# A three-stage fp32 network on one core: w1 loaded a second time for its sums, and fixed places for splits, sums and conversions

## The chip, the cores and the metric

The kernel runs on one core of one Trainium2 chip. Its engines are named as in the profile: PE (TensorE, matrix multiplication; PEld is its weight load), DVE (VectorE), ACT (ScalarE), POOL (GpSimd) and SP (SyncE, which issues most DMAs). Each engine works through its own queue in the order in which the program wrote the instructions, and waits on semaphores for the others. The metric is the device time in microseconds. Three runs before gave 1493.35 in the median (1492.63 to 1495.95).

## The reference: what is computed

Three layers follow one another, all in float32.

```python
# 1. attention, B=2, H=8, S=768, D=64; keep = first n_sink keys or a causal window of 128
scores = where(keep, q @ k.T / sqrt(D), -1e9)
x = softmax(scores) @ v                      # then rows of 8 heads side by side: x is 1536 x 512
# 2. mixture of E=8 experts, every token through each of them
P = exp(x @ w_gate - max); 8 times: P /= row sums, P /= column sums, P *= N/E
x = sum_e P[:, e] * (relu(x @ w1[e]) @ w2[e])     # w1[e] 512 x 1024, w2[e] 1024 x 512
# 3. one more two-layer network, d_ff = 2048; its weights arrive as 64-bit floats
out = (relu(x @ w_in) ** 2) @ w_out
```

## The kernel before

**Numbers.** Every float32 operand of a matmul is split in two parts, a high part in the type fp32r and the rest (lo = x - hi), and each product is three matmuls (hi x lo, hi x hi, lo x hi) that add up in one PSUM bank. `pair_split` (L428) makes a split: ACT copies to the high part, POOL subtracts.

**Chunks.** Behind attention, the two networks are 20 chunks of 512 hidden columns: chunk 0 is woven into attention, chunks 1 to 15 are the experts, 16 to 19 the last network. For a chunk, PE computes h = relu(x w1) for three blocks of 512 tokens (t = 0, 1, 2) and then adds h w2 into the accumulator `acc`. The order in PE's queue is: first products for t = 0 and 1; `second(c, 1)` (four groups of 12 matmuls); `plain(c, 2, f)` (four groups, the first products of t = 2); `second(c, 0)` and `second(c, 2)` (eight groups).

**Fast products.** Chunks 2 to 15 and 17 to 19 compute t = 0 and 1 with Strassen's scheme in Winograd's form (`fast`, L721): 7 products of 6 matmuls instead of 8, for each half of the chunk's columns, so 14 products p1, p6, p5, p2, p7, p3, p4, twice. It needs sums of w1's blocks (S1 to S4) and of x's blocks (T1 to T4, made once by `sums`, L604, for the experts and once for the last network). Within a half, p1's result is copied by ACT ("ts", L745), and DVE adds p6's to it ("tu"), p5's to that ("tz"), and so on (L737). p2 adds into the bank that "ts" has read, and p3 into the bank that "tz" has read, so PE waits for these two.

**Weights.** Raw weights come by DMA into a ring of three buffers of 512 KB (`rawp`), in the order of `load_list` (L388). A load is written into the queue as soon as the load three places ahead in the list has been used (`next_loads`, L400). A w1 half (`half_w1`, L432) is split in two steps into the tiles g0h, g0l (or g1h, g1l), then four POOL additions (L456) make the sums in place in the raw buffer, and two more splits follow. So the second splits wait for the sums, and the buffer is free only after them. `half_w2` (L466) does the two halves of w2.

**64-bit weights.** `wide` (L480) turns a piece of the last network's weights into float32: eight DVE operations (L491 to L519) on the tiles x0 and x1, and a DMA back to DRAM ("w<-x", L520). 32 pieces, three a chunk from chunk 2 on. L496, the second operation, writes x1, which the DMA of the piece before still reads.

**Order around the change.** All is written out by hand. `run` (L1197) takes a list of groups; after each group it takes `side` steps from a list of generators (`todo`) and some conversion steps, and after every second one a step of the gate (`gate`, L826). The w2 splits stand in the first groups of a chunk, the w1 splits of the next chunk in its last eight groups, two steps after each, and what is left over is written out at the end of the chunk. The conversion has three steps in two groups over the last 16 groups.

**Accumulation.** `add_up` (L574) adds a group's result into `acc` on DVE; in chunk 2 it multiplies `acc` by P first (L584). In the last chunk each tile of 128 tokens is stored right after it.

Of the kernel before, what the change touches and what calls it, by code (L numbers as in the profile page):

```python
# [2 lines left out]

# [15 lines left out]
DM = H * D  # L19
# [18 lines left out]
CONV = 3  # L38
NB = 512
# [5 lines left out]
class Kernel:  # L45
# [354 lines left out]
    def next_loads(self, *used):  # L400

        self.used.add(used)
        while self.lk < len(self.loads):
            if self.lk >= 3 and self.loads[self.lk - 3] not in self.used:
                return
            c, which, half = k = self.loads[self.lk]
            self.lk += 1
            if which == 2:
                raw = self.rawp.tile([128, 2 * FC], I32, tag="raw", name="raw64")
                w = (self.w1, self.w2)[c // 4 % 2][NC1 + c // 8]  # L410
                src = w[:, c % 4].bitcast(I32)
            else:
                w = self.w32[c - NC1, which] if c >= NC1 else (self.w1, self.w2)[which][c]
                if which == 0:
# [17 lines left out]
    def half_w1(self, c, half):  # L432

        nc = self.nc
        raw = self.loaded(c, 0, half)
        g = tuple(
            self.w1p.tile([128, 8, 2, 128], F32R, tag=f"g{half}{t}", name=f"g{half}{t}")
            for t in "hl"
        )
        self.W[c, half] = g  # L440
        parts = [
            tuple(x[:, k : k + 2].rearrange("p u k f -> p (u k) f") for x in g)
            for k in (0, 2, 4, 6)
        ]
        srcs = [raw[:, :, 0:128], raw[:, :, 128:256]]
        for k in range(2):
            self.pair_split(*parts[k], srcs[k])
            yield
        if self.is_fast(c):
            a11, a12 = raw[:, 0:2, 0:128], raw[:, 2:4, 0:128]  # L450
            a21, a22 = raw[:, 0:2, 128:256], raw[:, 2:4, 128:256]
            for o, x, y, op in (
                (a22, a21, a22, ALU.add), (a21, a11, a21, ALU.subtract),
                (a11, a22, a11, ALU.subtract), (a12, a12, a11, ALU.subtract),
            ):
                nc.gpsimd.tensor_tensor(out=o, in0=x, in1=y, op=op)  # L456
                yield
            for k in range(2):
                self.pair_split(*parts[2 + k], srcs[k])
                yield  # L460
        self.next_loads(c, 0, half)
# [4 lines left out]
    def half_w2(self, c, half):  # L466
        raw = self.loaded(c, 1, half)
        if half == 0:
# [3 lines left out]
        w = self.W[c, 2]  # L472
        for k in range(2):
            self.pair_split(w[0][:, 2 * half + k], w[1][:, 2 * half + k], raw[:, k])
            if k == 0:
                yield
        self.next_loads(c, 1, half)
        yield
# [95 lines left out]
    def add_up(self, c, ti, ps):  # L574

        nc = self.nc
        a = self.acc[:, ti, :]
# [13 lines left out]
        if c == NC - 1:  # L591
            nc.sync.dma_start(out=self.out[ti * 128 : (ti + 1) * 128, :], in_=a)
# [11 lines left out]
    def sums(self):  # L604
# [18 lines left out]
        for kc in range(2):  # L623
# [5 lines left out]
            yield  # L629
            x = tt("z", f32("B12", 0, kc), f32("B11", 0, kc), ALU.subtract)  # L630
# [87 lines left out]
    def weight(self, c, half, k):  # L718
        return tuple(x[:, k] for x in self.W[c, half])
# [63 lines left out]
    def second(self, c, t):  # L783

        def group(k):
            def go():
                s = slice(128 * k, 128 * k + 128)
                hh, hl = self.h[c, t]
                wh, wl = self.W[c, 2]
                ps = self.mmtile()  # L790
                n = 0
                for f in (0, 1, 3, 2):
                    for x, w in ((hh, wh), (hh, wl), (hl, wh)):
                        self.nc.tensor.matmul(  # L794
                            out=ps, lhsT=x[:, f, s], rhs=w[:, f], start=(n == 0), stop=(n == 11)
                        )
                        n += 1
                self.add_up(c, 4 * t + k, ps)
                self.finish()
            return go  # L800
# [169 lines left out]
    def reset(self):  # L970
# [6 lines left out]
        self.wr, self.W, self.h = {}, {}, {}  # L977
# [167 lines left out]
    def phase_b(self, c0, first, fill):  # L1145
# [27 lines left out]
        todo = [self.half_w1(c0, half) for half in range(2)]  # L1173

        def side_step():
            while todo:
                try:
                    return next(todo[0])
                except StopIteration:
                    todo.pop(0)  # L1180
# [6 lines left out]
        while todo:  # L1187
            side_step()
# [8 lines left out]
        def run(seq, side=1, conv=0):  # L1197
            for g in seq:
                g()
                for _ in range(side):  # L1200
                    side_step()
# [10 lines left out]
        for c in range(c0, NC):  # L1212
            if c == 2:
                for _ in gate:
                    pass
                self.steps = conv
            if not low:
                seq = [self.plain(c, 1, 0), *rest]
                run(seq)
# [9 lines left out]
            todo += [self.half_w2(c, half) for half in range(2)]  # L1229
# [3 lines left out]
            run(seq)  # L1233
            while todo:
                side_step()
            if c in (FAST - 1, FAST2 - 1):
                todo.append(self.sums())
            run(self.second(c, 1) + [self.plain(c, 2, f) for f in range(KD)], conv=3)
            if c + 1 < NC:
                todo += [self.half_w1(c + 1, half) for half in range(2)]  # L1240
            seq = self.second(c, 0) + self.second(c, 2)
            if c == NC1 - 1:
                x = [self.x2(t, kc) for t in (1, 0) for kc in range(KD)]
                seq = sum(([s, x[k]] for k, s in enumerate(seq)), [])
            run(seq, 2, 3)
            while todo:
                side_step()
# [94 lines left out]
```

## Time and profile before

| | |
|---|---|
| median of three runs | 1493.35 us |
| profiled execution | 1492.53 us, of which the span from the first to the last instruction 1490.7 us |
| PE busy | 1420.8 us (95%) |
| DVE busy | 848.1 us (57%) |
| POOL busy | 509.3 us (34%) |
| ACT busy | 449.0 us (30%) |
| mean granted clock of PE | 0.982 |
| read from HBM, written | 71.85 MB, 11.53 MB |

Matmuls are pipelined: the profile gives a matmul of 512 columns some 0.39 us, but the next one starts 0.23 us after it, so the distance between starts tells more than the length. PE counts as busy as long as one of them runs. The granted clock is a share of 2.4 GHz; 0.5 of it is the lower level, 1.2 GHz. A name such as "ts" or "hh" in a row is the tile that is written, without its buffer's number. In a row of a timeline, the brackets hold the idle time ahead of the instruction and what ended it.

### The profile page before, as it was taken

Reading aid. Unit: us, or ns where it says so; the run is one execution under the profiler, and the core shown is the slowest. Engines: PE = TensorE matmul, PEld = TensorE weight load, DVE = VectorE, ACT = ScalarE, POOL = GpSimd, SP = SyncE. Lnnn points to the kernel's source line nnn. Section 1 sums busy time; section 2 is a strip of 40 time slices with the busy share of each in tenths; the row PEclk is TensorE's granted clock in tenths of the full one; section 3 lists DMA queues with packets and bytes.
Section 4 is the critical chain, followed back from the end, with each engine's and each line's share of the span. In section 5 each row is a group of like instructions: output and inputs, shape, how many; then the busy total and the mean of one; then the engine's idle time right before and its main releaser. Section 6 shows DMA issues by size and latency. Waiting matters only on the chain.

```text
span 1490.7 us, 17219 instructions
## 1 busy us (share of the span) xinstructions
PE 1420.8 (95%) x6587; PEld 1169.5 (78%) x6587; DVE 848.1 (57%) x1567; ACT 449.0 (30%) x925; POOL 509.3 (34%) x461
## 2 busy tenths in 40 slices
PE   5799999999999999999999999999999999899998
PEld 4688888787778787878778787878888888678886
DVE  7978823866655546555565656554342446555352
ACT  5667622222221212122221212222122233334231
POOL 4534311535061423416152342515325021704320
PEclk9899999999999999999999999999999999999999
DMA  3322120012220312122131212212010010101001
GB/s 113 113 60 86 42 72 29 5 58 66 71 91 30 99 43 78 57 86 84 37 99 33 88 57 85 75 46 78 15 43 29 29 57 1 50 7 57 15 23 66
DMA packets 43181, 84.60 MB, mean 57 GB/s; under 512 B 3664, under 2 KB 25168, under 8 KB 42832
## 3 DMA queue, kind: packets, MB, share of 16 engines
q1 hardware_dynamic: 42800, 83.39, 17.6%
q8 instruction: 54, 0.88, 0.3%
q14 instruction: 39, 0.32, 0.1%
q10 hardware_dynamic: 288, 0.00, 0.0%
HBM read 71.85 MB, written 11.53 MB: 56 GB/s over the span
## 4 chain that ended last, share of the span: by engine, by line
PE 65%; DVE 13%; POOL 9%; DMA 6%; ACT 4%; issue 3%; ACTq 0%; DVEq 0%; SPq 0%; POOLq 0%
PE mm L794 28%; PE mm L696 27%; DMA raw<-w 5%; POOL raw L456 4%; POOL g1l L430 3%; PE xp L353 3%; POOL g0l L430 2%; PE mm L564 2%; PE mm L539 2%; DVE hl L674 1%; PE sc L225 1%; DVE hl L680 1%; DVE p L265 1%; DVE tx L668 1%; ACT hh L679 1%
## 5 line engine op out<-in xcount | busy, mean ns | idle before, releaser
L794 PE MATMUL mm<-w2h,hh 128*128 128x512 f32 x912 | 357.3, 392 | 0.8 <-ACT hh L679 0.8
L794 PE MATMUL mm<-w2h,hl 128*128 128x512 f32 x912 | 356.2, 391 | 0.0
L794 PE MATMUL mm<-w2l,hh 128*128 128x512 f32 x912 | 355.7, 390 | 0.0
L430 POOL TENSOR_TENSOR g0l<-raw,g0h 128x512 fp32r<-128x512 f32 x72 | 92.5, 1307 | 546.9 <-ACT g0h L429 546.9
L588 DVE SCALAR_TENSOR_TENSOR acc<-mm,P,acc 128x512 f32<-128x512 f32 x168 | 125.3, 746 | 173.7 <-PE mm L794 173.0
L794 PEld LDWEIGHTS mm<-w2h,hh 128*128 128x128 f32 x912 | 171.7, 188 | 37.2 <-ACT hh L679 2.1
L794 PEld LDWEIGHTS mm<-w2h,hl 128*128 128x128 f32 x912 | 171.5, 188 | 37.1 <-DVE hl L680 1.3
L794 PEld LDWEIGHTS mm<-w2l,hh 128*128 128x128 f32 x912 | 171.7, 188 | 35.4
L663 ACT ACTIVATE hh<-mm 128x512 fp32r<-128x512 f32 x96 | 57.2, 596 | 323.1 <-PE mm L696 323.1
L696 PE MATMUL mm<-xl,g1h 128*128 128x512 f32 x320 | 126.9, 397 | 20.5 <-ACT ts L745 20.4
L696 PE MATMUL mm<-xl,g0h 128*128 128x512 f32 x320 | 126.8, 396 | 11.3 <-ACT ts L745 6.9
L430 POOL TENSOR_TENSOR w2l<-raw,w2h 128x512 fp32r<-128x512 f32 x76 | 97.7, 1307 | 103.5 <-ACT w2h L429 103.5
L696 PE MATMUL mm<-xh,g0l 128*128 128x512 f32 x320 | 125.7, 393 | 0.0
L696 PE MATMUL mm<-xh,g0h 128*128 128x512 f32 x320 | 125.6, 393 | 0.0
L696 PE MATMUL mm<-xh,g1h 128*128 128x512 f32 x320 | 125.3, 392 | 0.0
L696 PE MATMUL mm<-xh,g1l 128*128 128x512 f32 x320 | 125.2, 391 | 0.0
L456 POOL TENSOR_TENSOR raw<-raw 128x256 f32<-128x256 f32 x136 | 120.5, 886 | 10.7
L430 POOL TENSOR_TENSOR g1l<-raw,g1h 128x512 fp32r<-128x512 f32 x72 | 96.8, 1365 | 69.0 <-ACT g1h L429 63.8
L674 DVE SCALAR_TENSOR_TENSOR hl<-mm,hh 128x512 fp32r<-128x512 f32 x96 | 65.8, 685 | 66.5 <-ACT hh L663 66.2
L429 ACT ACTIVATE g1h<-raw 128x512 fp32r<-128x512 f32 x72 | 41.5, 623 | 181.1 <-POOL raw L456 113.7
L696 PEld LDWEIGHTS mm<-xl,g1h 128*128 128x128 f32 x320 | 60.4, 189 | 37.8 <-ACT ts L745 24.7
L696 PEld LDWEIGHTS mm<-xl,g0h 128*128 128x128 f32 x320 | 60.6, 189 | 25.6 <-ACT ts L745 8.4
(199 smaller groups left out, 2400.4 us busy)
## 6 DMA issues: line engine op xcount, KB each, us to landing
raw<-w SPq DMA_DIRECT2D x76, 512.0 KB, 4.3
raw<-win SPq DMA_DIRECT2D x16, 512.0 KB, 4.8
w<-x SPq DMA_DIRECT2D x32, 256.0 KB, 4.5
raw<-wout SPq DMA_DIRECT2D x16, 512.0 KB, 5.3
raw<-qkv SPq DMA_DIRECT2D x8, 624.0 KB, 3.8
raw<-qkv SPq DMA_DIRECT2D x8, 464.0 KB, 3.5
out<-acc SPq DMA_DIRECT2D x12, 256.0 KB, 2.0
wraw<-w SPq DMA_DIRECT2D x2, 1024.0 KB, 7.8
```

Source lines behind the costliest of these rows:

```text
L225: nc.tensor.matmul(out=ps[:, 0:wd], lhsT=x[r, l * 128 : (l + 1) * 128], rhs=y[r, QW + off : QW + off + wd], start=(m == 0), stop=(m == 2),)
L353: nc.tensor.matmul(out=o, lhsT=l, rhs=r, start=(k == 0), stop=(k == last), skip_group_check=True)
L429: self.nc.scalar.activation(out=hi, in_=src, func=AF.Copy)
L430: self.nc.gpsimd.tensor_tensor(out=lo, in0=src, in1=hi.bitcast(F32), op=ALU.subtract)
L456: nc.gpsimd.tensor_tensor(out=o, in0=x, in1=y, op=op)
L539: nc.tensor.matmul(out=ps[:, 0:n], lhsT=w[:, kc, f * 128 : (f + 1) * 128], rhs=x[:, kc, t0 : t0 + n], start=(k == 0), stop=(k == 3 * KD - 1),)
L564: nc.tensor.matmul(out=ps, lhsT=x[:, f, s], rhs=w[:, f, :], start=(k == 0), stop=(k == 3 * KD - 1),)
L588: nc.vector.scalar_tensor_tensor(out=a, in0=ps, scalar=self.P[:, ti, e : e + 1], in1=a, op0=ALU.mult, op1=ALU.add)
L663: nc.scalar.activation(out=hh, in_=src, func=AF.Relu)
L674: nc.vector.scalar_tensor_tensor(out=hl, in0=src, scalar=0.0, in1=hh.bitcast(F32), op0=ALU.max, op1=ALU.subtract,)
L696: self.nc.tensor.matmul(out=ps, lhsT=w[:, kc], rhs=x[:, kc], start=start and k == 0, stop=(k == n - 1), skip_group_check=True,)
L794: self.nc.tensor.matmul(out=ps, lhsT=x[:, f, s], rhs=w[:, f], start=(n == 0), stop=(n == 11))
```

## The change

Raw w1 of a fast chunk is loaded twice. One copy (kind 3 in the list of loads) is turned into sums by POOL (`unit_sums`) and split into tiles of its own (s0, s1); the other (kind 0) is split into the plain tiles (a0, a1). The loads have a new order, in which those of the next chunk stand between the conversion's. The generators and `todo` are gone: a plan names after which group each split, sum and conversion step is written into the queues. With m groups of first products (14 in a fast chunk), the sums of the next chunk's w1 stand after groups m to m+3, their splits after m+4 to m+7, the plain splits after m+9, m+10, m+12 and m+13, the conversion's steps, two each, after m+0 to m+3 and m+6 to m+13; the splits of the chunk's own w2 after groups 2, 5, 8 and 11. The gate's steps have places in a list, the sums of x start with the chunk's first groups, with T3 for both halves first. The very last tile of the last chunk is computed, added up and stored in two halves of 256 columns.

The diff, cut to its core:

```diff
+CONV_AT = (0, 1, 2, 3, 6, 7, 8, 9, 10, 11, 12, 13)
+GATE_AT = (0, 1, 2, 3, 5, 7, 9, 11, 13, 16, 19, 22, 25, 28)
+W2_AT = (2, 5, 8, 11)
...
     def load_list(self, c0):
-        loads, k = [], 0
+        loads, k = [(c0, which, half) for which in range(2) for half in range(2)], 0
         for c in range(c0, NC):
-            loads += [(c, which, half) for which in range(2) for half in range(2)]
-            if c >= 2:
-                for _ in range(CONV):
-                    if k < 8 * NC2:
-                        loads.append((k, 2, 0))
-                        k += 1
+            wide = [(j, 2, 0) for j in range(k, min(k + CONV, 8 * NC2)) if c >= 2]
+            k += len(wide)
+            n = c + 1
+            loads += wide[0:1]
+            if n < NC:
+                if self.is_fast(n):
+                    loads += [(n, 3, 0), (n, 3, 1)]
+                loads += wide[1:2] + [(n, 0, 0)] + wide[2:3] + [(n, 0, 1), (n, 1, 0), (n, 1, 1)]
...
+    def units(self, c, half, which, k):
+        if k == 0:
+            n = f"{'as'[which // 3]}{half}"
+            self.W[c, half, which] = tuple(
+                self.w1p.tile([128, 4, 2, 128], F32R, tag=n + t, name=n + t) for t in "hl"
+            )
+            self.half[c, which, half] = self.loaded(c, which, half)
+        raw = self.half[c, which, half]
...
+        self.pair_split(hi, lo, raw[:, :, 128 * k : 128 * k + 128])
+        if k == 1:
+            del self.half[c, which, half]
+            self.next_loads(c, which, half)
+
+    def unit_sums(self, c, half, k):
+        raw = self.loaded(c, 3, half)
+        self.wr[c, 3, half] = raw
...
+        for o, x, y, op in jobs[2 * k : 2 * k + 2]:
+            self.nc.gpsimd.tensor_tensor(out=o, in0=x, in1=y, op=op)
...
+    def part_w2(self, c, k):
...
+                cuts = 2 if (c, t, k) == (NC - 1, 2, 3) else 1
+                for i in range(cuts):
+                    d = slice(DM // cuts * i, DM // cuts * (i + 1))
...
+                    self.add_up(c, 4 * t + k, ps, d)
...
+        def run(seq, plan):
+            for k, g in enumerate(seq):
                 g()
-                for _ in range(side):
-                    side_step()
-                k = next(groups)
-                for _ in range((k * conv + conv) // 2 - k * conv // 2):
-                    next(self.steps, None)
-                if k % 2 == 0:
+                for step in plan.get(k, ()):
+                    step()
+                if next(groups) in GATE_AT:
                     next(gate, None)
...
+            for k in range(4):
+                put(W2_AT[k] if self.is_fast(c) else k, self.part_w2, c, k)
...
+                wide = lambda k: m + k
+            if c in (FAST - 1, FAST2 - 1):
+                t = self.sums()
+                for k in range(13):
+                    put(*((k, next, t, None) if c < FAST else (2 * k, next, t, None)))
+            if c + 1 < NC:
+                if self.is_fast(c + 1):
+                    for half in range(2):
+                        for k in range(2):
+                            put(wide(2 * half + k), self.unit_sums, c + 1, half, k)
+                            put(wide(4 + 2 * half + k), self.units, c + 1, half, 3, k)
+                for half in range(2):
+                    for k in range(2):
+                        put(wide(9 + 3 * half + k), self.units, c + 1, half, 0, k)
+            if c > 1:
+                for k in CONV_AT:
+                    put(wide(k), next, conv, None)
+                    put(wide(k), next, conv, None)
+            run(seq, plan)
```

## Rows read from the trace of the kernel before

**Rows 1.** Chain that ended last, in order of time: start, length (us), what.

```profile
320.10 10.88 PE mm L794 x48
...
388.67 10.88 PE mm L794 x48
...
981.24 10.88 PE mm L794 x48
...
1168.92 10.88 PE mm L794 x48
```

**Rows 2.** Stretches: start:end, length, engines' busy times, PE's clock, DMA share, GB/s.

```profile
250.00:300.00 50.00, 47.05 (x207) 38.50 (x207) 40.24 (x82) 11.56 (x20) 22.39 (x20) 0.97 0.03 11
1100.00:1150.00 50.00, 50.00 (x223) 41.39 (x222) 16.53 (x25) 9.28 (x16) 16.02 (x16) 1.00 0.06 17
1250.00:1300.00 50.00, 42.71 (x179) 34.26 (x178) 26.76 (x36) 16.22 (x30) 28.04 (x26) 0.93 0.06 20
```

**Rows 3.** What PE waited for: line, releaser: us in total, times, longest.

```profile
PE mm L696 <- ACT ts L745: 27.3, 11, 6.0
...
PE mm L696 <- DVE tz L737: 4.4, 1, 4.4
PE mm L878 <- DVE P L873: 3.0, 1, 3.0
...
PE mm L794 <- ACT hh L679: 0.8, 3, 0.3
```

**Rows 4.** Timelines of SP, ACT and PE, 635 to 646: start, length, instruction.

```profile
635.44 0.33 SPq L420 DMA_DIRECT2D raw<-w  x1
...
639.82 0.63 ACT L429 ACTIVATE w2h<-raw 128x512 fp32r<-128x512 f32 x1 [5.00 <-DMA raw<-w]
...
644.99 0.58 ACT L745 ACTIVATE ts<-mm 128x512 f32<-128x512 f32 x1
...
643.35 0.39 PE L696 MATMUL mm<-xh,g1l 128*128 128x512 f32 x1
645.63 0.50 PE L696 MATMUL mm<-xl,g1h 128*128 128x512 f32 x1 [1.89 <-ACT ts L745]
```

**Rows 5.** What DVE waited for, and two rows of its timeline.

```profile
DVE x L496 <- DMA w<-x: 107.8, 21, 8.5
...
598.18 0.68 DVE L510 SCALAR_TENSOR_TENSOR x<-x,raw 128x512 int32<-128x512 int32 x1
...
612.38 1.12 DVE L510 SCALAR_TENSOR_TENSOR x<-x,raw 128x512 int32<-128x512 int32 x1
```

**Rows 6.** DVE's timeline in chunk 2 and where chunk 3 starts.

```profile
340.83 0.48 DVE L584 TENSOR_SCALAR acc<-acc,P 128x512 f32<-128x512 f32 x1
...
368.93 1.51 DVE L584 TENSOR_SCALAR acc<-acc,P 128x512 f32<-128x512 f32 x1
```

**Rows 7.** Groups of instructions by shape: busy us, mean ns | idle before, releaser.

```profile
L588 DVE SCALAR_TENSOR_TENSOR acc<-mm,P,acc 128x512 f32<-128x512 f32 x168 | 125.3, 746 | 173.7 <-PE mm L794 173.0
...
L456 POOL TENSOR_TENSOR raw<-raw 128x256 f32<-128x256 f32 x136 | 120.5, 886 | 10.7
...
L430 POOL TENSOR_TENSOR g1l<-raw,g1h 128x512 fp32r<-128x512 f32 x72 | 96.8, 1365 | 69.0 <-ACT g1h L429 63.8 <-PE mm L794 5.1
...
L519 DVE TENSOR_TENSOR x<-x,x 128x512 f32<-128x512 f32 x32 | 24.0, 751 | 0.4
...
L737 DVE TENSOR_TENSOR tu<-mm,ts 128x512 f32<-128x512 f32 x34 | 23.3, 686 | 28.4 <-ACT ts L745 15.2 <-PE mm L696 13.2
...
L491 DVE TENSOR_SCALAR x<-raw 128x512 int32<-128x512 int32 x32 | 18.3, 573 | 0.7
```

**Rows 8.** DMA issues: count, KB each, median us from issue to landing.

```profile
raw<-w SPq DMA_DIRECT2D x76, 512.0 KB, 4.3
...
w<-x SPq DMA_DIRECT2D x32, 256.0 KB, 4.5
```

**Rows 9.** Timelines: two matmuls of 256 columns, and the last instruction of DVE.

```profile
168.01 0.28 PE L353 MATMUL xp<-ptl,vh 128*128 128x256 f32 x1
168.13 0.28 PE L353 MATMUL xp<-pth,vh 128*128 128x256 f32 x1
...
1484.73 0.69 DVE L581 TENSOR_TENSOR acc<-mm,acc 128x512 f32<-128x512 f32 x1 [2.03 <-PE mm L794]
```

More of the change, by code (lines that the diff above doesn't have):

```diff
@@ L2 @@
 from contextlib import ExitStack
+from functools import partial
 import concourse.bass as bass
@@ L430, in pair_split @@
         self.nc.gpsimd.tensor_tensor(out=lo, in0=src, in1=hi.bitcast(F32), op=ALU.subtract)
[L432 to L438, printed above, removed]
-        )
[L440 to L461, printed above, removed]
@@ new lines, in units @@
+    def units(self, c, half, which, k):
[6 more added lines that the diff above has]
+        raw = self.half[c, which, half]
+        hi, lo = (
+            x[:, 2 * k : 2 * k + 2].rearrange("p u k f -> p (u k) f")
+            for x in self.W[c, half, which]
+        )
+        self.pair_split(hi, lo, raw[:, :, 128 * k : 128 * k + 128])
+        if k == 1:
+            del self.half[c, which, half]
+            self.next_loads(c, which, half)
@@ L471, in half_w2 @@
             )
[L472 to L478, printed above, removed]
+        if j == 0:
+            self.half[c, 1, half] = self.loaded(c, 1, half)
+        w, raw = self.W[c, 2], self.half[c, 1, half]
+        self.pair_split(w[0][:, k], w[1][:, k], raw[:, j])
+        if j == 1:
+            del self.half[c, 1, half]
+            self.next_loads(c, 1, half)
     def wide(self, k):
@@ L591, in add_up @@
         if c == NC - 1:
[L592 removed]
+            nc.sync.dma_start(out=self.out[ti * 128 : (ti + 1) * 128, d], in_=a)
     def operand(self, name):
@@ L629, in sums @@
             yield
+        for kc in range(2):
             x = tt("z", f32("B12", 0, kc), f32("B11", 0, kc), ALU.subtract)
@@ L718, in weight @@
     def weight(self, c, half, k):
-        return tuple(x[:, k] for x in self.W[c, half])
+        return tuple(x[:, k % 4] for x in self.W[c, half, k // 4 * 3])
     def fast(self, c, half):
@@ L789, in go @@
                 wh, wl = self.W[c, 2]
[L790 to L798, printed above, removed]
+                cuts = 2 if (c, t, k) == (NC - 1, 2, 3) else 1
+                for i in range(cuts):
+                    d = slice(DM // cuts * i, DM // cuts * (i + 1))
+                    ps = self.mmtile()
+                    n = 0
+                    for f in (0, 1, 3, 2):
+                        for x, w in ((hh, wh), (hh, wl), (hl, wh)):
+                            self.nc.tensor.matmul(
+                                out=ps[:, d], lhsT=x[:, f, s], rhs=w[:, f, d], start=(n == 0),
+                                stop=(n == 11),
+                            )
+                            n += 1
+                    self.add_up(c, 4 * t + k, ps, d)
                 self.finish()
@@ L1172, in phase_b @@
         nc.sync.dma_start(out=wgr, in_=self.wg)
[L1173 to L1180, printed above, removed]
+        todo = [partial(self.units, c0, half, 0, k) for half in range(2) for k in range(2)]
         for _ in fill:
@@ L1184, in phase_b @@
                 self.evac()
-                side_step()
+                if todo:
+                    todo.pop(0)()
         self.evac()
-        while todo:
-            side_step()
+        for step in todo:
+            step()
         hz = self.wgz[:, :, 0:E]
@@ L1213, in phase_b, with put @@
             if c == 2:
-                for _ in gate:
-                    pass
                 self.steps = conv
+            plan = {}
+            def put(k, *step):
+                plan.setdefault(k, []).append(partial(*step))
+            off = 0
             if not low:
-                seq = [self.plain(c, 1, 0), *rest]
-                run(seq)
+                run([self.plain(c, 1, 0), *rest], {})
                 low = first.close() or True
@@ L1232, in phase_b @@
                 seq = sum(([s, *x[k : k + 1]] for k, s in enumerate(seq)), [])
[L1233 to L1241, printed above, removed]
+            m = len(seq)
+            seq = seq + self.second(c, 1) + [self.plain(c, 2, f) for f in range(KD)]
             if c == NC1 - 1:
                 x = [self.x2(t, kc) for t in (1, 0) for kc in range(KD)]
[L1244 to L1247, printed above, removed]
+                seq += sum(
+                    ([s, x[k]] for k, s in enumerate(self.second(c, 0) + self.second(c, 2))), []
+                )
+                wide = lambda k: m + k if k < 8 else m + 2 * k - 8
+            else:
+                seq += self.second(c, 0) + self.second(c, 2)
+                wide = lambda k: m + k
[17 more added lines that the diff above has]
+            run(seq, plan)
         left.close()
```

28 lines of the change are left out of this document (16 added, 12 removed).

## The prediction

> **What bounds the kernel now.** I read four views in this order: the chain that ended last in order of time, what TensorE (PE) waited for, the stretches, and then the timelines of single engines. The times of the whole are 1490.7 us of span in a profiled execution of 1492.53 us; the three runs have a median of 1493.35, 0.8 above it.
>
> In the chain the reader is to compare starts. The row "L794 x48" is the first part of each chunk's second matmul, so the distance from one to the next is a chunk's length [rows 1]. From 981.24 to 1168.92 three chunks take 187.68, 62.56 each; a chunk has 276 matmuls of 512 columns, so that is 62.56 / 276 = 0.2267 each, and in a stretch there PE is never idle and its granted clock is 1.00 [rows 2]. This is the floor, and the change removes no matmul. But from 320.10 to 388.67 (chunk 3) it takes 68.57, which is 6.0 more, and the nine chunks from 388.67 to 981.24 take 592.57 instead of 563.04: 29.5 more, 3.3 each. Chunks 13 to 15 are those in which no 64-bit weights are converted any more.
>
> What PE waited for names the places [rows 3]: eleven waits for the copy "ts" on ACT (27.3 us, the longest 6.0), one of 4.4 for VectorE's (DVE) "tz" at the start of chunk 3, one of 3.0 for the gate. Each wait costs more than its row: the gap from 643.35 to 645.63 is 2.28, so 2.05 over the 0.2267 for a row of 1.89 [rows 4], and after some the clock is lower for a few us: in 1250 to 1300, where chunk 17 starts, PE is busy 42.71 of 50 at a mean clock of 0.93, so 7.3 + 0.07 x 50 = 10.8 are lost; with the gate, in 250 to 300, 2.95 + 0.03 x 50 = 4.5 [rows 2]. All in all 6.0 + 29.5 + 10.8 + 4.5 = 50.8 us could be gained, and 0.8 at three waits for "hh" in chunks 17 to 19.
>
> Why PE waits is read from ACT's timeline [rows 4]: its queue is in order, "ts" of the second half (644.99) stands behind the split of w2's second half, which waited 5.0 for its load; that load went out at 635.44 at the earliest, when the raw buffer came free from the late w1 splits. So: w1 of the next chunk is split in the last 8 groups, w2's load waits for its buffer, ACT waits for w2's load, PE for ACT.
>
> **The change part by part.** *Load order and w1 twice.* Each of the 17 fast chunks gets two more loads of 512 KB, 34 in all; such a load lands in 4.3 [rows 8], on the DMA queues, while their stretches show a DMA share of 0.03 to 0.06 [rows 2] and the rest of the span stays far from full. Walking through the new list with its three buffers, I find that both w2 loads of a chunk are issued in the chunk before, after groups j10 and j11 (j counts the 16 groups of 2.72 that follow the 14 fast products of 1.36, which end 19.04 after the chunk's start). They have landed before ACT reaches them, at group 2. That takes away the wait of [rows 4]. Value: the nine chunks get 29.5 back, minus what the next parts cost. It costs nothing on SyncE's queue but 34 issues of 0.33 [rows 4].
>
> *Sums in their own tiles.* Instructions on GpSimd (POOL) and ACT stay the same in number: 8 sums of 0.89 and 8 splits of 1.31 to 1.37 a chunk [rows 7], 17.8 us on POOL. Before, they start with the last 8 groups (21.8 us) and run over into the next fast products; now they start with j0, with 43.5 us. S tiles are free from the end of the fast products, plain tiles after j5 and j7, and the last split is put at j13, two groups (5.4) before its use; ACT and POOL run ahead of PE, as nothing in their queues there depends on it but four relus. In chunk 17 the same spread removes the 10.8; I leave 0.5, so 10.3 gained.
>
> *w2 splits at groups 2, 5, 8, 11* instead of 0 to 3. The last is the tight one: ACT's 0.6 and POOL's 1.3 begin behind group 11, at 16.3 plus some 1.6 for the product's sum and relu, and end near 19.9; PE asks for this quarter's low part at 19.04 + 7 x 0.2267 = 20.6. Margin 0.7: cost 0, at most 1 a chunk.
>
> *Conversion in fixed places.* This is the part that could give it back. DVE works in order; a wide piece is eight operations, from 0.57 (first) to 0.75 (last), 5.3 in sum with the means of the six between them [rows 7]. The second operation waits until the piece before has been written out (4.5 [rows 8]); before, these waits sum to 107.8, the longest 8.5 [rows 5]. In a steady chunk two calls stand after each place, but the last operation of a piece and the first of the next come in one call, so pieces change at j2, at j8 and, with a place left empty after j11, at j13. From the second change: j8 ends at 43.5; add_up 0.75, a "hl" 0.68 and the last operation put the write at 45.7, landed at 50.7 with issue; then one short operation (0.4), three add_ups of 0.75 [rows 7] and the operations 3 to 7 (3.5): 56.8. Now two transfers and a write go out behind one another; the next piece's load at about 58.2, landed 62.5. Operations 1 and 2 (1.1) and two add_ups (1.5) are done at 65.1, and the next chunk's "u" and "z" (0.69 each [rows 7]) at 66.5; PE's products allow "z" at 67.5 at the earliest, and p3, which overwrites what "z" reads, is due at 62.56 + 6.80 = 69.4. So DVE has 2.9 to spare. If POOL is at work, its neighbour on DVE is slower where it reads SBUF alone: L510 took 0.68 at 598 and 1.12 at 612 [rows 5], L584 0.48 and 1.51 [rows 6]. I leave 3 in total for chunks 4 to 12 (bounds 0 and 40, below): 26.5 gained.
>
> The Trainium skill goes further here: SBUF — State Buffer, section Terms, says that VectorE and GpSimd share a port pair by an exclusive lock held for a whole instruction, so that the loser is blocked fully. L510's 0.44 more, beside POOL instructions of 0.89 and 1.31, is less than a whole one, and the add_ups, which read PSUM, keep 0.75; the trace agrees with the sharing, not with its full size. By that rule the two POOL splits that fall between j8 and j11 would cost DVE up to 2.6, nearly all of the 2.9. The sum doesn't change, but it is a reason to give the first rival 0.22 rather than half of that.
>
> *Chunk 2 into chunk 3.* Here twelve L584 come on top, 0.48 to 1.51 each [rows 6], and the pieces change one call later, so that operation 7 falls to j12. 2.7 (a group) + 1.2 (L584 on the way, beyond what waits hide) + 1.5 (three more behind j13) = 5.4 later, minus 2.9: 2.5 of wait stay of 6.0 (bounds 0 and 6.0). Gain 3.5.
>
> *Gate and sums of x in chunk 1.* Both are put from the chunk's first groups on, where DVE was little used, instead of both in 250 to 300, where it is busy 40.24 of 50 [rows 2]. I leave 1 of 4.5 (bounds 0 and 4.5): 3.5. *Last tile in halves.* 24 matmuls of 256 columns at 0.12 [rows 9] are 2.88 instead of 12 x 0.2267 = 2.72; the last addition, 0.69 [rows 9], is halved. 0.2 less, and a smaller last store: 0.3 gained (bounds -0.2 and 0.6).
>
> Sum: 26.5 + 10.3 + 3.5 + 3.5 + 0.3 = 44.1. 1492.5 - 44.1 = 1448.4 for a profiled execution, 1449.2 as a median with the 0.8 above.
>
> **Rivals.** *1. The piece at the chunk's boundary.* "u" and "z" stand behind operation 1, which waits for a load. If write and load each take 2 us longer than their medians, as three transfers at a time may make them, 4 - 2.9 = 1.1 of wait, and about 1.5 for the lower clock behind it (a fall like that of chunk 17 gave 3.5, a gap of 2.05 with none gave 0): 2.6 in nine chunks is 23, of which 3 is counted, so 1469. For it: the 107.8 and the 8.5 [rows 5]. Against it: medians of 4.3 and 4.5 [rows 8].
>
> *2. w2's last quarter comes too late.* If the split behind group 11 is 1.7 late, PE waits 1 in 17 chunks: 1466. For it: a margin of 0.7. Against it: in chunks 13 to 15 nothing waits there with the same matmuls.
>
> *3. Slower than before.* The same place as rival 1, with both transfers at the longest wait, 8.5, in every chunk from 4 to 12: 8 later, 5.1 of wait plus 1.5 is 6.6 a chunk, 59 in nine; with chunk 3's gain gone too: 1449 + 56 + 3.5 = 1508. It decides from 1449 + 44 on, at 47 / 9 = 5.2 a chunk. Against it: 21 waits make the 107.8, a mean of 5.1.
>
> *4. The change doesn't do what it says:* ACT still waits for loads ahead of "ts" and half of the 29.5 + 10.8 stays, 1470. Against it: the new order of loads.
>
> **How the numbers follow.** The forecast has 0.60 (its own range 1443 to 1457), rival 1 0.22 (1457 to 1480), rival 2 0.06, rival 4 0.04, rival 3 0.04, and 0.04 that all waits go, 1441. I say 1449, with 1443 to 1468: it takes in the forecast and the half of the first two rivals that lies below it. A measurement of this kernel tells some 0.2% from no change, 3 us: faster 0.93, within it 0.02, slower 0.05.
>
> **What would show it.** In the chain the distances of "L794 x48" rows should be 62.6 to 63 from chunk 4 on and about 65 for chunk 3; among PE's waits "ts" should be gone, "tz" stay once; ACT should have no wait for a w2 load, and the longest wait of DVE should be for a raw load (L491). If "tz" or "tu" come in every chunk to 12, rival 1 is right; if "w2l" or "w2h" does, rival 2. A chunk of 65 without a wait that a row names would make the reading of the floor wrong.

## The result, and the profile after

The changed kernel takes 1447.62 us in the median of four runs (1446.48 to 1448.24), the kernel before 1494.65 beside it (1492.63 to 1496.32): 0.9685 of the time, with a 95% interval of 0.9668 to 0.9702. The profiled execution took 1446.48, 1.9 less than the 1448.4 forecast for it. The page of the changed kernel:

```profile
span 1444.7 us, 17358 instructions
...
HBM read 89.67 MB, written 11.53 MB: 70 GB/s over the span
```

The span is 46.0 us shorter, though 17.8 MB more are read. The next rows are from its chain that ended last (start, length, what); what was L794 is now L806, and L696 is L705:

```profile
311.70 2.73 PE mm L806 x12
...
376.20 10.88 PE mm L806 x48
...
939.24 10.88 PE mm L806 x48
...
1126.91 10.88 PE mm L806 x48
...
1209.02 10.88 PE mm L705 x48
...
1274.01 10.88 PE mm L705 x48
...
1340.63 10.88 PE mm L705 x48
...
1404.52 10.88 PE mm L705 x48
```

Read the distances, beside those of [rows 1]. Chunks 4 to 12 now take 939.24 - 376.20 = 563.04: nine times the floor of 62.56 (the time of a chunk in which PE never waits), to the hundredth. Chunk 3 takes 64.50 instead of 68.57. Chunks 13 to 15 are at 62.56 as before. The last four rows are the first products for t = 2 of chunks 16 to 19: 64.99, 66.62 and 63.89 apart, where before chunks 18 and 19 took 63.52 and 63.51. So more is lost there than before.

What PE waited for, beside [rows 3]:

```profile
PE mm L806 <- ACT hh L688: 2.8, 3, 1.1
...
PE mm L705 <- DVE tz L746: 1.6, 1, 1.6
...
PE mm L806 <- DVE hl L689: 1.1, 2, 0.6
```

In the same three columns (total, times, longest), a wait of ACT in the kernel before, for w2:

```profile
ACT w2h L429 <- DMA raw<-w: 54.5, 10, 6.1
```

After the change, ACT's longest wait for weights, and two of DVE's for the conversion:

```profile
ACT a1h L437 <- DMA raw<-w: 61.0, 13, 7.1
...
DVE x L499 <- DMA raw<-wout: 37.1, 11, 4.3
...
DVE x L504 <- DMA w<-x: 27.2, 10, 3.4
```

The eleven waits for "ts" and the gate's are gone, one for "tz" is left, and ACT's 54.5 us for the loads of w2 are gone too. DVE's 107.8 for the write of a converted piece [rows 5] have become 27.2, and the raw loads come first, as foretold. ACT still waits 61.0 for w1's loads, but no wait of PE stands behind them. New are the longer "hh" and the "hl".

The span's 46.0 us (rounded terms below), from the chains of both profiled executions, against the 44.1 forecast:

| where | forecast | measured | from |
|---|---|---|---|
| attention, code unchanged | 0 | 3.6 | start of L539/L547 x48: 204.35, 200.78 |
| chunk 1: gate and sums of x | 3.5 | 4.8 | from there to the first matmul of `second(2, 1)`: 115.75, 110.92 |
| chunk 3 | 3.5 | 4.1 | 68.57, 64.50 |
| chunks 4 to 12 | 26.5 | 29.5 | 592.57, 563.04 |
| start of chunk 17 | 10.3 | 10.5 | 1251.03 to 1325.02 before: 73.99, less 62.56 and the 0.96 of chunks 18, 19 |
| POOL's work beside chunks 17 to 19 | 0 | -4.9 | 195.50 after, 3 x 62.56 + 3 x 0.96 without |
| last tile, and the stretch behind PE's last matmul | 0.3 | -1.5 | matmuls +0.2; last matmul to the end 6.40, 7.67 |

### The profile page after: what moved, and what is told of

Same layout as the page of the kernel before. It is cut to its first block, busy times and chain, and to the rows that moved or that the text cites. A ratio compares the mean times of both kernels' runs of the same rounds, so it can differ in the third digit from the quotient of the medians.

```text
span 1444.7 us, 17358 instructions
## 1 busy us (share of the span) xinstructions
PE 1405.2 (97%) x6599; PEld 1163.5 (81%) x6599; DVE 906.1 (63%) x1568; ACT 448.2 (31%) x925; POOL 526.5 (36%) x461
## 4 chain that ended last, share of the span: by engine, by line
PE 86%; DVE 9%; ACT 2%; DMA 2%; issue 1%; SPq 0%; ACTq 0%; DVEq 0%
PE mm L806 41%; PE mm L705 36%; PE xp L357 2%; PE mm L572 2%; PE mm L547 2%; DVE p L269 1%; PE sc L229 1%; DVE hl L689 1%; PE ptp L282 1%; DVE tx L677 1%; DVE p L242 1%; ACT hh L688 1%; DMA raw<-win 1%; DVE st L259 1%; ACT qkh L184 1%
## 5 line engine op out<-in xcount | busy, mean ns | idle before, releaser
L806 PE MATMUL mm<-w2h,hh 128*128 128x512 f32 (+1 forms) x916 | 357.8, 391 | 2.8 <-ACT hh L688 2.8
L806 PE MATMUL mm<-w2h,hl 128*128 128x512 f32 (+1 forms) x916 | 356.6, 389 | 1.1 <-DVE hl L689 1.1
L806 PE MATMUL mm<-w2l,hh 128*128 128x512 f32 (+1 forms) x916 | 356.4, 389 | 0.0
L806 PEld LDWEIGHTS mm<-w2h,hh 128*128 128x128 f32 x916 | 172.3, 188 | 39.0 <-ACT hh L688 4.0
L806 PEld LDWEIGHTS mm<-w2h,hl 128*128 128x128 f32 x916 | 172.4, 188 | 38.1 <-DVE hl L689 2.4
L806 PEld LDWEIGHTS mm<-w2l,hh 128*128 128x128 f32 x916 | 172.5, 188 | 35.2
L705 PE MATMUL mm<-xl,a0h 128*128 128x512 f32 x252 | 98.6, 391 | 0.0
L705 PE MATMUL mm<-xl,a1h 128*128 128x512 f32 x252 | 98.5, 391 | 0.0
L705 PE MATMUL mm<-xh,a0l 128*128 128x512 f32 x252 | 98.1, 389 | 0.0
L705 PE MATMUL mm<-xh,a0h 128*128 128x512 f32 x252 | 98.1, 389 | 0.0
L705 PE MATMUL mm<-xh,a1h 128*128 128x512 f32 x252 | 98.1, 389 | 0.0
L705 PE MATMUL mm<-xh,a1l 128*128 128x512 f32 x252 | 98.1, 389 | 0.0
L438 POOL TENSOR_TENSOR a1l<-raw,a1h 128x512 fp32r<-128x512 f32 x38 | 50.2, 1342 | 45.4 <-ACT a1h L437 39.1
```

Source lines behind the costliest of these rows:

```text
L438: self.nc.gpsimd.tensor_tensor(out=lo, in0=src, in1=hi.bitcast(F32), op=ALU.subtract)
L705: self.nc.tensor.matmul(out=ps, lhsT=w[:, kc], rhs=x[:, kc], start=start and k == 0, stop=(k == n - 1), skip_group_check=True,)
L806: self.nc.tensor.matmul(out=ps[:, d], lhsT=x[:, f, s], rhs=w[:, f, d], start=(n == 0), stop=(n == 11),)
```

## The experiments

**before_x1_two.** The kernel before, in which the second tile of the conversion alternates between two, so that a piece needn't wait until the one before has been written out.

```diff
-        x, m = (self.xp_.tile([128, FC], I32, tag=t, name=t) for t in ("x0", "x1"))
+        x, m = (self.xp_.tile([128, FC], I32, tag=t, name=t) for t in ("x0", ("x1", "x2")[k % 2]))
```

> The kernel before, but the conversion's tile x1 takes turns with x2, so that the second operation of a piece (L496) needn't wait until the piece before is written out. Theory A (PE's waits for 'ts' come from ACT standing behind w2's late load): DVE's wait of 107.8 for 'w<-x' falls under 30, chunk 3 gains up to 6.0, but the waits for 'ts' stay in chunks 4 to 12, with at most 5 of the 29.5 gained: 1484 to 1493. Rival B (DVE's waits in the conversion are what holds ACT and PE up, and the fixed places of the conversion removed them): most of the 29.5 goes with them, 1458 to 1470.

1480.39 against 1490.26 before: 0.9935 [0.9917, 0.9952]. Its waits of PE and ACT, and its chain:

```profile
PE mm L696 <- ACT ts L745: 25.3, 12, 6.0
...
PE mm L696 <- DVE tz L737: 0.8, 1, 0.8
...
ACT w2h L429 <- DMA raw<-w: 53.4, 10, 5.9
```

```profile
316.50 10.88 PE mm L794 x48
...
381.26 10.88 PE mm L794 x48
...
968.36 10.88 PE mm L794 x48
```

The 107.8 us of DVE's waits are gone, and "tz" falls from 4.4 to 0.8: chunk 3 takes 64.76, which is 3.8 less. But "ts" stays, and chunks 4 to 12 still take 587.10, 5.5 less than before and 24.1 over the floor. Theory A has the kind right, but its range, 1484 to 1493 with at most 5 of the 29.5 gained, is missed by 3.6. So DVE's largest wait was worth some 9 us of its 107.8, and most of the loss in the middle has another cause; the next run takes that one away.

**before_w2_spread.** The kernel before with one thing of the change: the splits of w2 stand after groups 2, 5, 8 and 11 instead of 0 to 3. Loads, sums and conversion are as before.

```diff
...
-                for _ in range(side):
+                for _ in range(side if at is None or i in at else 0):
...
-            run(seq)
+            run(seq, at=(2, 5, 8, 11) if self.is_fast(c) else None)
```

> One part of the change alone, on the kernel before: in the fast chunks the four w2 splits stand after groups 2, 5, 8 and 11 instead of 0 to 3. Theory A2 (the 3.3 a chunk are ACT waiting for w2's second load; the load lands about 7.5 into the chunk, which is ahead of group 8 at 12.2): the waits for 'ts' in chunks 4 to 12 go, 20 to 29 of the 29.5 are gained, chunk 3 and chunk 17 stay as they are: 1461 to 1473 where before has 1493. Rival C (it needs the second copy of w1 and its own tiles): at most 5 gained, 1485 or more.

1463.91 against 1490.69: 0.9813 [0.9783, 0.9844]. Chain and PE's waits:

```profile
318.80 10.88 PE mm L794 x48
...
389.62 10.88 PE mm L794 x48
...
953.75 10.88 PE mm L794 x48
```

```profile
PE mm L696 <- ACT ts L745: 6.7, 2, 6.0
...
PE mm L696 <- DVE tz L737: 5.5, 1, 5.5
...
PE mm L878 <- DVE P L873: 3.0, 1, 3.0
```

From 389.62 to 953.75 are 564.13, 1.1 over the floor: this alone gives back 28.4 of the 29.5. Chunk 3 takes 70.82 instead of 68.57, so the whole kernel gains 26.8. What stays are the three waits at single places: chunk 17's "ts" (6.0), chunk 3's "tz", the gate's "P".

**w2_early.** The changed kernel with the splits of w2 put back to groups 0 to 3.

```diff
-W2_AT = (2, 5, 8, 11)
+W2_AT = (0, 1, 2, 3)
```

> The kernel after with the w2 splits back after groups 0 to 3 in all fast chunks; all else as after. Theory A2: w2's loads are out 18 and more before the chunk starts, so ACT doesn't wait and chunks 4 to 12 stay at 62.56; in chunks 17 to 19 POOL has no w2 split beside DVE's last operations of the first products, and the losses there (2.2, 2.2 and 1.1 at the start of the second matmul) fall to 0.3 to 1.0 each: 2 to 5 less than after. Rival D (these places are what removed the waits for 'ts'): they come back in chunks 4 to 12, 2 to 3 each, 20 to 30 more than after.

1445.48: 0.9696 [0.9664, 0.9729], not to be told from the change. Chunks 4 to 12 stay at the floor (375.88 to 938.91). So with the rest of the change the old places do no harm in these chunks: splitting w2 later is one remedy, the rest of the change, whose w2 loads ACT no longer waits for, is another, and each is enough. The 2 to 5 us that theory A2 expected from the last network didn't come. There the waits only move: "hh" is back to 0.9 in three, but "ts" has 2.2 in two and "tz" 2.1 in two at the starts of second halves, and chunks 17 and 18 take 66.19 each; chunks 17 to 19 together take 195.91, as long as in the change.

**late_splits.** The changed kernel with sums and w1 splits of the next chunk as late as before the change: sums after m+8 and m+9, splits in the six groups behind them.

```diff
-                            put(wide(2 * half + k), self.unit_sums, c + 1, half, k)
-                            put(wide(4 + 2 * half + k), self.units, c + 1, half, 3, k)
+                            put(wide(8 + half), self.unit_sums, c + 1, half, k)
+                            put(wide(10 + half), self.units, c + 1, half, 3, k)
...
-                        put(wide(9 + 3 * half + k), self.units, c + 1, half, 0, k)
+                        put(wide(12 + half), self.units, c + 1, half, 0, k)
```

> The kernel after with w1 loaded twice into tiles of its own, but all of it written into the queues after j8 to j13, two or four steps a group, as near the chunk's end as before. Theory A: POOL's 17.8 begin at 43.5 instead of 20 and end near 62, the plain copies and w2 are requested late, so w2's second load lands only 2 to 5 into the next chunk; ACT stands behind it or PE waits for a split: 0.5 to 2.5 a chunk in 14 chunks, 1455 to 1482. Rival C (the second copy and its own tiles are enough by themselves): 1446 to 1451.

1442.93: 0.9673 [0.9638, 0.9708]. Chain, and ACT's longest wait for weights:

```profile
313.17 10.88 PE mm L806 x48
...
375.73 10.88 PE mm L806 x48
...
938.76 10.88 PE mm L806 x48
```

```profile
ACT a0h L437 <- DMA raw<-w: 119.3, 12, 11.1
```

Theory A's 1455 to 1482 is missed. Rival C is right in kind; the time is even below its 1446 to 1451, but the kernel before is faster here too (1490.26, not 1494.65). ACT waits 119.3 us for loads, up to 11.1 at a time, and no chunk from 3 to 15 is above 62.56: the waits stand where PE needs nothing of ACT. The earlier start of sums and splits, which I had made a condition, isn't one; chunk 3 takes 62.56 without it and 64.50 with it.

**one_load.** The changed kernel with w1 loaded once: plain splits after m+6 to m+9, sums in place, their splits behind, and the loads in an order that fits. The places of w2 and of the conversion's steps stay, and so do the tiles of the sums.

```diff
-            loads += wide[0:1]
+            loads += wide[0:2]
...
-                if self.is_fast(n):
-                    loads += [(n, 3, 0), (n, 3, 1)]
-                loads += wide[1:2] + [(n, 0, 0)] + wide[2:3] + [(n, 0, 1), (n, 1, 0), (n, 1, 1)]
+                loads += [(n, 0, 0), (n, 0, 1)] + wide[2:3] + [(n, 1, 0), (n, 1, 1)]
...
```

> The kernel after, but w1 is loaded once, as before, and its sums are made in place; the plain splits stand after j6 to j9, the sums after j8 and j10, the sums' splits after j9, j10, j12 and j13; tiles of their own, everything in fixed places, and the load order fitted to seven loads a chunk. Theory A (what counts is that every split is done and w2's loads are out before the chunk's end): no waits for 'ts' in chunks 4 to 12, 1446 to 1453. Rival C (the second copy of w1 is what makes room): w2's second load goes out only behind the last split, ACT stands behind it in the first products again, 2 to 3 a chunk: 1472 to 1490.

1458.06: 0.9776 [0.9743, 0.9809], and no theory's number. PE's and DVE's waits:

```profile
PE mm L703 <- DVE tz L744: 13.0, 10, 9.2
...
DVE x L497 <- DMA raw<-win: 39.7, 6, 6.9
```

"ts" doesn't come back, but a buffer is held longer, so the conversion's raw load goes out late and DVE's queue stands: 9.2 at chunk 3 (313.53 to 387.00 is 73.47, 10.9 over the floor) and 0.3 to 0.5 at each of the nine chunks behind (569.41, 6.4 over). This is rival 1's mechanism, set off by a late load instead of a long one. This kernel is 1458.06 - 1447.62 = 10.4 slower than the change, on another chip; its chain loses 10.9 + 6.4 - 1.9 = 15.4 more in chunks 3 to 12. Since places and order changed with the copy, this is the price of one arrangement, not of the second copy alone. What it does show is that "ts" goes without a second copy.

**conv_even.** The changed kernel with the conversion spread as before, three steps in two groups.

```diff
-                for k in CONV_AT:
-                    put(wide(k), next, conv, None)
-                    put(wide(k), next, conv, None)
+                for k in range(16):
+                    for _ in range((3 * k + 3) // 2 - 3 * k // 2):
+                        put(wide(k), next, conv, None)
```

> The kernel after, but the conversion's 24 steps are spread evenly, three in two groups, over the chunk's last 16 groups as before. Theory A: DVE has some 3 us to spare at the chunk's boundary, so chunks 4 to 12 stay within 1 us of 62.56, chunk 3 may lose 1 to 3: 1446 to 1456. Rival B: waits for 'tz' or 'tu' at the start of chunks 3 to 12, 1.5 to 4 each: 1463 to 1485.

1442.02: 0.9678 [0.9643, 0.9714]. Chunks 4 to 12 take 563.04 (374.86 to 937.90), and "tz" at chunk 3 is 1.1. Like late_splits it lies below its theory's range, beside the same faster kernel before. The fixed places of the conversion are worth nothing here.

**w2_last and late_w2_last.** The splits of w2 go back to groups 0 to 3 in the last network alone, in the changed kernel and in late_splits.

```diff
-                put(W2_AT[k] if self.is_fast(c) else k, self.part_w2, c, k)
+                put(W2_AT[k] if FAST <= c < NC1 else k, self.part_w2, c, k)
```

> The kernel after with the w2 splits after groups 0 to 3 in chunks 17 to 19 alone. Theory E (DVE's operations on SBUF alone are slowed while POOL works beside them: 1.22 and 1.02 instead of 0.69): with w2's splits and the sums behind them over by about 16 into the chunk, these take 0.69 again and the losses fall from 5.4 in sum to 1 to 3. Rival F (it is ACT's extra copy in that place, or the two more DVE operations that the last network's activation needs): the losses stay above 4.

> Sums and splits of w1 after j8 to j13 as in the run with late splits, and the w2 splits of chunks 17 to 19 after groups 0 to 3. Theory E: no loss in chunks 2 to 16 and 1 to 3 in 17 to 19, so 2 to 4 below the run with late splits: a ratio of 0.964 to 0.966 to before. Rival F: the same as with late splits, 0.967.

1446.76, 0.9705 [0.9674, 0.9735], and 1446.08, 0.9698 [0.9664, 0.9733]. "hh" falls to 0.9 and 0.8 in three, but "ts" takes 2.2 and 3.7 in its place, and "tz" 2.2 in two and 1.1. The gain that I expected didn't come: in w2_last chunks 17 to 19 take 195.95. POOL, which has no w2 to wait for later, runs on into the sums, and these lie beside the middle of the fast products instead of their end. That left the theory unproved: POOL's work beside DVE, or ACT's copies themselves?

**sums_behind.** late_splits with early w2 in the last network, and for chunks 18 and 19 the sums behind the plain splits, so that POOL has nothing to run ahead with.

```diff
...
+                if n > FAST2:
+                    loads += [(n, 0, 0), (n, 0, 1), (n, 3, 0), (n, 3, 1), (n, 1, 0), (n, 1, 1)]
+                    continue
...
+                        put(wide(6 + 2 * half + k if last else 12 + half), self.units, c + 1, half, 0, k)
...
+                        put(wide(8 + 2 * half + k), self.unit_sums, c + 1, half, k)
+                        put(wide(10 + 2 * half + k), self.units, c + 1, half, 3, k)
...
```

> Sums and splits after j8 to j13 for chunks up to 17; for chunks 18 and 19 the plain copies of w1 are loaded and split first and the sums' copies behind them, so that POOL's sums can't run ahead into the first products of 17 and 18 (the plain tiles come free only after j5 and j7); w2's splits of chunks 16 to 19 after groups 0 to 3. Theory E (POOL beside DVE's operations on SBUF is what made the waits in 17 and 18): waits for 'ts' and 'tz' there 0.3 at most, 'hh' about 0.3 three times, 0.9 lost a chunk at most; together with chunk 3 some 4 to 6 less than after: ratio 0.962 to 0.967. Rival F (the last network's longer activation makes them by itself): 1.5 to 2.5 stay in 17 and 18, 2 less than after at most.

1439.13 against 1492.95 before: 0.9651 [0.9632, 0.9670], 8.3 below the changed kernel on the same chip. Its chain at chunks 17 to 19, PE's only waits there, and DVE in chunk 17 (L692 and L680 are L689 and L677 of the change):

```profile
1205.29 10.88 PE mm L708 x48
...
1269.67 10.88 PE mm L708 x48
...
1333.21 10.88 PE mm L708 x48
...
1396.74 10.88 PE mm L708 x48
```

```profile
PE mm L708 <- ACT ts L757: 0.2, 1, 0.2
...
PE mm L809 <- ACT hh L691: 0.9, 3, 0.3
```

```profile
1258.19 0.69 DVE L692 TENSOR_TENSOR hl<-tx,hh 128x512 fp32r<-128x512 f32 x1
1258.85 0.69 DVE L680 SCALAR_TENSOR_TENSOR tx<-txq,tx 128x512 f32<-128x512 f32 x1
```

The chunks take 64.38, 63.54 and 63.53. POOL does nothing from 1250 to 1266, and DVE's instructions are at 0.69. The rival, that ACT's copies of w2 or the last network's longer activation cost it, is wrong: both are as in late_w2_last, and the waits are gone. ACT makes no split of a sum in these stretches (from 1243 to 1268 in the change its rows are w2's splits, "ts", "tx" and "hh"), so POOL's work is left, and the lengths of DVE's instructions, below, say how it acts.

Chunks 17 to 19 take 191.45 here, and 195.50, 193.86 and 195.50 in the profiled executions of the change, after_again and whole_tail, so sums_behind saves 4.05 or 2.41 there, and about 1.9 at chunk 3 (309.90 to 372.46). Not all of the 8.3 is its doing: between the profiled executions of after_again and sums_behind, 10.0 apart, attention makes 4.7 and the end 0.9, and both vary between executions. Its median is the lowest of all kernels here, but its interval overlaps those of late_splits and conv_even.

**after_again and whole_tail.** The changed kernel once more, and with its last tile whole.

```diff
-                cuts = 2 if (c, t, k) == (NC - 1, 2, 3) else 1
+                cuts = 1
```

> The kernel after once more, unchanged, on one chip beside the next two. Its losses should stand in the same places: 1.9 where chunk 3 starts, 2.2, 2.2 to 3.7 and 1.1 where the second matmuls of chunks 17 to 19 start, none in chunks 4 to 12. What attention takes should differ from the profile before, since the same code took 199.9 to 204.4 in the profiles so far: 1441 to 1449, with a ratio of 0.966 to 0.971.

> The kernel after with its last tile in one piece, as before. By the prediction's term the two halves save 0.3: from the start of the last group's first matmul to the end of the span 0.3 longer than after. From the two profiles on hand (6.4 from the last matmul's start to the end before, 7.7 after, and 5.7 to 6.0 in two other runs with halves) the halves save 0.2 to 0.6 and the 7.7 is chance. The time differs by less than 1 us either way.

1447.42, 0.9692 [0.9671, 0.9713], and 1447.19, 0.9701 [0.9686, 0.9717]: no difference. From the last matmul's start to the end it is 7.27 and 7.58.

## Why the prediction was right, point by point

**The loss and its floor: right.** 0.2267 a matmul and 62.56 a chunk were reached in nine chunks. The cause, too: ACT's queue, in order, with "ts" behind a split that waits for a load. before_w2_spread shows it for chunks 4 to 12, as its edit moves these splits and nothing else.

**Load order and w1 twice: the effect was right, its credit too wide.** I gave it the 29.5. The place of the w2 splits, which I had costed at 0 as a mere risk, gives 28.4 of them by itself; the rest of the change gives all of them without it (w2_early). No run has the new order of loads alone, and one_load is free of "ts" without the second copy. 26.5 was short by the 3 that I had left for the conversion, and none of these were needed.

**Sums from j0 on: not needed.** Chunk 17's start was gained (10.5 for 10.3), but late_splits gains it with late sums too. Nor is it the place of w2, which leaves the 6.0 of "ts" there (before_w2_spread), nor the second copy (one_load has no "ts"). ACT's timeline in the kernel before shows what stood ahead of that "ts":

```profile
1277.22 0.63 ACT L429 ACTIVATE Th<-tq 128x512 fp32r<-128x512 f32 x1 [1.95 <-DVE tq L641]
...
1293.93 1.15 ACT L429 ACTIVATE g1h<-raw 128x512 fp32r<-128x512 f32 x2 [6.73 <-POOL raw L456]
```

"ts" follows at 1294.99. It is not a load of w2 that holds the queue here: the splits of w1 come behind the last sums of x ("Th"), 26.2 after chunk 16's products for t = 2 begin, and then wait for POOL's sums in the raw buffer. The change also moved the sums of x to the chunk's first groups, gave w1's sums tiles of their own and put loads and splits in a new order. All kernels with the change have these three, and no run tells them apart, so which of them gave the 10.5 stays open.

**w2's last quarter: right in chunks 4 to 15.** Chunk 4 starts at 482.28 - 62.56 = 419.72 by the first product of chunk 5. The low part comes on POOL:

```profile
500.59 1.85 POOL L438 TENSOR_TENSOR w2l<-raw,w2h 128x512 fp32r<-128x512 f32 x1 [4.56 <-ACT w2h L437]
```

It ends at 502.44, 20.16 after the start of chunk 5, whose w2 it is; I had 19.9, and a need at 20.6. The margin was 0.4, not 0.7, and it held. Rival 2 didn't occur.

**Conversion at the boundary: right.** DVE at the start of chunk 5 (start, length, instruction, and the idle time ahead):

```profile
482.34 0.42 DVE L504 TENSOR_SCALAR x<-raw 128x512 int32<-128x512 int32 x1
...
486.39 0.69 DVE L746 TENSOR_TENSOR tz<-mm,tu 128x512 f32<-128x512 f32 x1 [0.60 <-PE mm L705]
```

Counted from chunk 4's start, the second operation ends at 63.0 (I had 63.6), "z" at 67.4 (67.5), and the bracket says that DVE stood idle for 0.60 ahead of it until PE's product came. Transfers didn't grow longer with 34 loads more:

```profile
raw<-w SPq DMA_DIRECT2D x110, 512.0 KB, 3.8
...
w<-x SPq DMA_DIRECT2D x32, 256.0 KB, 3.6
```

They were 4.3 and 4.5 [rows 8]. So rivals 1 and 3 had no ground in this kernel; one_load, whose loads go out later, shows rival 1. The change did what it says (rival 4).

**Chunk 3: right in kind and size.** 1.6 of wait stay, for the 2.5 that I left; with later sums and splits they go too (late_splits).

**Gate and sums in chunk 1: right, sized a little low.** The stretch that answers to the first of [rows 2]:

```profile
250.00:300.00 50.00, 50.00 (x228) 41.39 (x228) 33.00 (x68) 10.57 (x19) 25.51 (x22) 1.00 0.14 43
```

PE has no gap left in it, so the 1 us that I kept back came too. The 4.8 is 0.3 above my upper bound, about what the clock's rounding to two places makes in 50 us (0.25). That the new places did it is by subtraction: every kernel with them has lost this wait, and before_w2_spread, without them, has it.

**The term that was wrong: POOL's moved work beside chunks 17 to 19, put at nothing.** I had the w2 splits at groups 2, 5, 8 and 11 as "cost 0, at most 1 a chunk", argued for chunks 13 to 15, and let POOL run ahead with its sums without a price. Both hold where PE has a margin. In chunks 17 to 19 the fast products' ends are tighter: before, PE waited there 0.3 for each "hh", and I left these 0.8 unchanged, without asking what the moved POOL work lies beside. The place of w2 by itself isn't it, as w2_early and w2_last lose as much with the old one. DVE and POOL in chunk 17 of the changed kernel, then PE:

```profile
1261.15 1.02 DVE L689 TENSOR_TENSOR hl<-tx,hh 128x512 fp32r<-128x512 f32 x1
1262.09 1.22 DVE L677 SCALAR_TENSOR_TENSOR tx<-txq,tx 128x512 f32<-128x512 f32 x1
1263.24 0.68 DVE L746 TENSOR_TENSOR tq<-mm,tu 128x512 f32<-128x512 f32 x1
1264.01 1.25 DVE L689 TENSOR_TENSOR hl<-tx,hh 128x512 fp32r<-128x512 f32 x1
```

```profile
1260.32 1.30 POOL L438 TENSOR_TENSOR w2l<-raw,w2h 128x512 fp32r<-128x512 f32 x1 [2.74 <-ACT w2h L437]
1261.58 5.43 POOL L469 TENSOR_TENSOR raw<-raw 128x256 f32<-128x256 f32 x5
```

```profile
1264.03 0.50 PE L806 MATMUL mm<-w2h,hh 128*128 128x512 f32 x1 [1.12 <-ACT hh L688]
...
1265.32 0.50 PE L806 MATMUL mm<-w2h,hl 128*128 128x512 f32 x1 [0.55 <-DVE hl L689]
```

While POOL runs, from 1260.32 on, the instructions of DVE whose operands are all in SBUF take 1.02 to 1.25 instead of 0.69; "tq", which reads a PSUM bank ("mm"), keeps 0.68. The same holds from 1200 to 1410: of the rows of "hl" and "tx" with both inputs in SBUF, the 21 beside an idle POOL take 0.68 to 0.70, the 27 beside a working one 1.13 on the mean, and the 33 DVE rows that read PSUM beside a working one 0.68 to 0.69. Each "hh" comes from a "tx", so the chain to PE grows by 0.3 to 0.6 a step. The gaps of PE make 2.43 in chunk 17 (64.99 over 62.56), 4.06 in 18, 1.33 in 19, which has no sums behind it; 2.9 of the 7.8 were there before. after_again has 65.01, 64.98 and 63.87, so 1.6 of the change's chunk 18 is not in every execution, and the term is -3.3 there instead of -4.9. sums_behind shows the cause by taking it away: what is left in chunks 17 to 19 is 3.8 over the floor.

In the prediction I set a rule of the Trainium skill against [rows 5, 6]. The same page of the Trainium skill, SBUF — State Buffer, says in section "🔬 SBUF: two separate sides" that a VectorE instruction with two SBUF inputs and a GpSimd instruction that reads SBUF lock each other out for a whole instruction. These rows agree on which instructions suffer; the additions are 0.33 to 0.56, beside POOL instructions of about 1.09 (5.43 / 5). That would fit a wait until a running one ends, somewhat less than half of one on the mean, but no row shows the wait itself. I had used the rule for the boundary of chunks 4 to 12, where it cost nothing, and not for the last network, where it did.

**The last tile: not measurable.** The matmuls of 256 columns cost the 0.2 that was forecast, and the last addition takes 0.42 instead of 0.69. But the end behind them goes from 6.40 to 7.67 here, and over the thirteen profiled executions from 5.7 to 7.7, halves and whole alike.

**Not forecast: 3.6 in attention.** The change leaves its instructions as they are. In the stretch from 50 to 100 us PE's granted clock is 0.86 before and 0.92 after the change. after_again, the same kernel as the change, has 0.85 there, and its attention takes 203.67 instead of 200.78: so at least 2.9 of the 3.6 is what two executions of one kernel differ by, and I count the whole as chance. So the total came nearer to the forecast than its terms deserve: +3.6 by chance, +5.1 from terms sized too low, -4.9 beside POOL and -1.8 for the tail make, rounded, the 1.9 more. That it came within 2 us is luck; that chunks 4 to 12 reached the floor is not.

## What to carry to other kernels

On an engine that works in order, ask of each instruction that waits for a load what is queued behind it: moving the four w2 splits of a chunk to where their loads have landed gave 28.4 us in chunks 4 to 12, and new loads with all else gave the same, so that either remedy hid the other. A long wait off the path may be worth little (some 9 us for DVE's 107.8) or nothing (ACT's 119.3), so take it away alone before building on it. And when work moves on an engine that nothing holds back, look at what it will now run beside: POOL's splits and sums lengthened DVE's SBUF instructions by half to four fifths, at a place where PE had no margin.

## What the runs showed that I had not expected

Attention has the same code in all kernels here, but the row of 48 matmuls that ends it starts anywhere from 199.0 to 204.4 us in the thirteen profiled executions; that is 5.4 us that a single profile can't tell from a change. And a short gap of PE is sometimes followed by a lower clock and sometimes not: the same gaps at the same place of chunk 18 (1.09 and 0.56 us, 1.11 and 0.55) made 66.62 in one execution of the changed kernel and 64.98 in the other. In the first the granted clock is 0.66 in the four us from 1330, where eight matmuls start 0.43 apart instead of 0.23, the pace of the lower level (1.2 GHz); in the other it is 1.00 from 1331.3 to 1335.3.
